# Retention and a two-layer PReLU network on one core: first batch in chunks of 128 tokens, second batch with one block of products for each pair of heads

## The chip, the cores and the metric

The kernel runs on one core of a Trainium2 chip. A core has TensorE (matrix products, written to PSUM banks), VectorE, ScalarE, GpSimd and a queue engine that starts transfers; they run beside each other and wait for one another by semaphores. The metric is the device time of one execution in microseconds. Everything is in fp32.

## What is computed

Eight batches, eight heads, 576 tokens of 64 values. Each head's attention is a retention: scores that decay with the distance of the tokens, nothing above the diagonal. Its output is laid out as 4608 tokens of 512 values and goes through a network of 512 to 2048 to 512 with a leaky activation whose slope is different for each of the 2048 features.

```python
scores = q @ k.T / sqrt(64)                      # per batch and head, 576 x 576
gamma = 1 - 2.0 ** (-5 - h)
ret = scores * where(i >= j, gamma ** (i - j), 0)
x = (ret @ v)                                    # (8, 576, 8 * 64) -> 4608 x 512
h = x @ w_in                                     # 4608 x 2048
g = maximum(h, 0) + alpha * minimum(h, 0)
out = g @ w_out                                  # 4608 x 512
```

The retention is computed by chunks: inside a chunk by masked scores, and from earlier chunks through a running state, the sum of decayed k times v of each chunk (64 x 64 for each head).

## The kernel before

Batch 0 has its own path. It is cut into three parts, of 256, 256 and 64 tokens; a part of 256 tokens has four chunks of 64. All heads of a part are done together: transposes, scores, states, values. Here `c` is a pair of heads, `h2` a head of the pair, `m` one of two blocks of 128 tokens, and `p2` a chunk in the block. `half(x)` is partitions 64x to 64x + 63, `chunk(j)` is columns 64j to 64j + 63. q and k are scaled beforehand so that decay inside a part is a mere mask.

```python
def part_scores(x):
    ...
    banks = part_banks(x, 2 if x == 0 else None, "ps")
    for m in range(2):
        for c in range(NPAIR):
            for p2 in range(2):
                for h2 in range(2):
                    j = chunk(2 * m + p2)
                    nc.tensor.matmul(banks[h2][half(p2), (2 * c + m) * C:(2 * c + m + 1) * C],
                                     kT[half(h2), c, j], qT[half(h2), c, j], start=True, stop=True)
    # part 0: VectorE multiplies both banks by the mask; part 1: ScalarE copies, GpSimd masks

def part_states(x):            # four states of 64 tokens
    for m, c, p2, h2 in ...:
        nc.tensor.matmul(banks[p2][half(h2), m, c], kn[half(p2), m, 2 * c + h2],
                         vn[half(p2), m, 2 * c + h2], ...)
    # running sums over j = 0..3: part 0 by ScalarE copies and GpSimd, part 1 by VectorE

def part_values(x):
    for m, c, p2, h2 in ...:   # own chunk
        nc.tensor.matmul(banks[p2][half(h2 ^ p2), c, m], vn[half(p2), m, 2 * c + h2],
                         at[half(p2), h2, n * C:(n + 1) * C], ...)
    for j in range(1 if x == 0 else 0, 4):      # earlier chunks, in two halves of 32 partitions
        for c, h2, e in ...:
            nc.tensor.matmul(banks[j % 2][to:to + 32, c, j // 2],
                             su[half(h2), c, e:e + 32], qT[half(h2), c, chunk(j)], ...)
    # ScalarE copies to xb: for each j parity, the odd chunks with their heads swapped
```

After part 0 come filler products (`idle`), a small transpose for the slopes, and then the first unit of the network. A unit is 2 x 128 of the 2048 features for a block of 256 tokens: a first product `ph` (eight matmuls of 256 columns), the activation by ScalarE and VectorE, and a second product `po` (four matmuls of 512 columns). The first two blocks of tokens use this plain form; the others use seven products in place of eight (Strassen). The weights are rounded as they arrive, in 32 pieces, each with two operations of ScalarE, three of VectorE and one of GpSimd (`piece_in`, `piece_out`).

```python
idle = ps_h.tile([P, DM], FP32, tag="psh0", name="idle")
for _ in range(2):
    nc.tensor.matmul(idle, ident, part[0][0][:, 0]..., start=True, stop=True)
...                                             # slopes, weight pieces
plain_unit(0, 0)                                # ph of block 0, unit 0
plain_relu()
```

The pairs of heads of batch 1 (four pairs, n = 4 to 7) are spread over twelve plain units, in small steps between the units' products: "s" scores, "u" states and their running sums, "w" the copy of the sums, "p" scaling, "v" values, "t" transposes on VectorE.

```python
def pair_scores(n, kT, qT):
    ps = [ps_tile([P, NM, C], f"ps{p2}_{n}") for p2 in range(2)]
    for j in range(NJ):                         # nine chunks
        for h2 in range(2):
            nc.tensor.matmul(ps[j % 2][half(x), j // 2], kT[half(h2), chunk(j)], qT[half(h2), chunk(j)], ...)
    # ScalarE copies qT beside the scores, VectorE applies decay and mask
def pair_states(n, kn, vn):
    ps = [ps_tile([P, NM - 1, D], f"pu{p2}_{n}") for p2 in range(2)]
    for j in range(NJ - 1):
        for h2 in range(2):
            nc.tensor.matmul(ps[j % 2][half(x), j // 2], kn[half(1 - h2), j], vn[half(1 - h2), h2, j], ...)
    return running_sums(n, *ps)

for n, (kb, i) in enumerate(units):
    plain_unit(kb, i); plain_relu()
    if n >= 1: gap()                            # the next of the steps
    piece_in(1); piece_out(1)
    mlp_out()                                   # po of the unit before
    ...
    piece_in(1)
    if n >= 2: gap()
    piece_out(1)
```

Later batches do a pair in one block, `joint`: the values of the pair before, then `pair_front`, scores and states of eight chunks into two PSUM banks together, with the ninth chunk's scores in a bank of the values (`extra`).

Of the kernel before, what the change touches and what calls it, by code (L numbers as in the profile page):

```python
# [18 lines left out]
def kernel(  # L19
# [121 lines left out]
    def room(i, s0, n):  # L141
# [8 lines left out]
        ((5, 4), (5, 5), (5, 6), (6, 4)), ((6, 5), (6, 6), (7, 4), (7, 5)), ())]  # L150
# [32 lines left out]
    mask = const.tile([P, C], FP32, name="mask")  # L183
    nc.gpsimd.memset(mask, 1.0)
    for p2 in range(2):
        nc.gpsimd.affine_select(out=mask[p2 * C:(p2 + 1) * C], in_=mask[p2 * C:(p2 + 1) * C],
                                compare_op=ALU.is_ge, fill=0.0, base=0, pattern=[[1, C]],
                                channel_multiplier=-1)
# [208 lines left out]
    def plain_out(kb, i, g, between):  # L397
# [3 lines left out]
        for x in range(2):  # L401
            if x and between:
                between()
            for m in range(2):
                nc.tensor.matmul(acc[kb][m], g[:, 2 * x + m],  # L405
                                 w_out[i][:, 2 * x:2 * x + 2].rearrange("p x f -> p (x f)"),
                                 start=(i == 0 and x == 0), stop=(i == NU - 1 and x == 1))
# [140 lines left out]


    def pair_scores(n, kT, qT):  # L550
        c = pairs[n][1]

        mt = attn.tile([P, 2 * S], FP32, tag="at", name=f"mt_{n}").rearrange(
            "p (h j s) -> p h j s", h=2, s=C)
        ps = [ps_tile([P, NM, C], f"ps{p2}_{n}") for p2 in range(2)]
        for j in range(NJ):
            for h2 in range(2):
                x = (1 - h2, h2)[j % 2]
                nc.tensor.matmul(ps[j % 2][half(x), j // 2], kT[half(h2), chunk(j)],  # L559
                                 qT[half(h2), chunk(j)], start=True, stop=True)  # L560
        for h2 in range(2):
            nc.scalar.copy(mt[half(h2), h2].rearrange("p j s -> p (j s)"), qT[half(h2)])
        for p2 in range(2):
            for h2 in range(2):
                h, to, x = 2 * c + h2, half(1 - h2), (1 - h2, h2)[p2]
                nm = NM - p2
                nc.vector.scalar_tensor_tensor(
                    out=mt[to, h2, p2::2], in0=ps[p2][half(x), 0:nm], scalar=th[to, 3, h:h + 1],
                    in1=mask[to, None, :].to_broadcast([C, nm, C]), op0=ALU.mult, op1=ALU.mult)
        return mt  # L570

    def pair_states(n, kn, vn):
        ps = [ps_tile([P, NM - 1, D], f"pu{p2}_{n}") for p2 in range(2)]
        for j in range(NJ - 1):
            for h2 in range(2):
                x = (h2, 1 - h2)[j % 2]
                nc.tensor.matmul(ps[j % 2][half(x), j // 2], kn[half(1 - h2), j],  # L577
                                 vn[half(1 - h2), h2, j], start=True, stop=True)
        return running_sums(n, *ps)

# [22 lines left out]

    later = []

    def pair_front(n, kT, qT, kn, vn, extra):
# [20 lines left out]
        for h2 in range(2):  # L627
            to = half(1 - h2)
            nc.vector.scalar_tensor_tensor(  # L629
                out=mt[to, h2, NJ - 1], in0=extra[to],  # L630
                scalar=th[to, 3, 2 * c + h2:2 * c + h2 + 1], in1=mask[to],
                op0=ALU.mult, op1=ALU.mult)
        for p2 in range(2):
            for h2 in range(2):
# [4 lines left out]
                    in1=mask[to, None, :].to_broadcast([C, NM - 1, C]),  # L639
                    op0=ALU.mult, op1=ALU.mult)  # L640
        later.append(lambda: pair_sums(vn, running_sums(n, ps[0][:, 1], ps[1][:, 1])))
# [61 lines left out]

    def part_scores(x):
        at = tat[x] = (mlp.tile([P, 8 * P], FP32, tag="g", name=f"pa_{x}") if x == 0 else
                       room(4, 0, 4)).rearrange("p (h n) -> p h n", h=2)
        banks = part_banks(x, 2 if x == 0 else None, "ps")
        kT, qT = tT[x, 0], tT[x, 1]
        for m in range(2):
            for c in range(NPAIR):  # L710
                for p2 in range(2):
                    for h2 in range(2):
                        j = chunk(2 * m + p2)
                        nc.tensor.matmul(banks[h2][half(p2), (2 * c + m) * C:(2 * c + m + 1) * C],  # L714
                                         kT[half(h2), c, j], qT[half(h2), c, j],
                                         start=True, stop=True)
        for h2 in range(2):
            to, fro = [t.rearrange("p (n s) -> p n s", s=C) for t in (at[:, h2], banks[h2])]
            m = mask[:, None, :].to_broadcast([P, 8, C])
            if x == 0:  # L720
                nc.vector.tensor_tensor(out=to, in0=fro, in1=m, op=ALU.mult)
            else:
                nc.scalar.copy(to, fro)
                nc.gpsimd.tensor_tensor(out=to, in0=to, in1=m, op=ALU.mult)

    def part_states(x):
        kn, vn = part[x][0], part[x][2]
        banks = [t.rearrange("p (m c d) -> p m c d", m=2, c=NPAIR)
                 for t in part_banks(x, None if x == 0 else 0, "pu")]
        for m in range(2):  # L730
            for c in range(NPAIR):
                for p2 in range(2):
                    for h2 in range(2):
                        nc.tensor.matmul(banks[p2][half(h2), m, c], kn[half(p2), m, 2 * c + h2],  # L734
                                         vn[half(p2), m, 2 * c + h2],
                                         start=(m == 0 and c == 0),
                                         stop=(m == 1 and c == NPAIR - 1), skip_group_check=True)
        was = carry[x]
        for j in range(4):
            u = banks[j % 2][:, j // 2]  # L740
            if x == 0:
                nc.scalar.copy(sums[x][j], u)
                if j:
                    nc.gpsimd.tensor_tensor(out=sums[x][j], in0=was, in1=sums[x][j], op=ALU.add)
            else:
                nc.vector.tensor_tensor(out=sums[x][j], in0=was, in1=u, op=ALU.add)
            was = sums[x][j]

    def part_carry(x):
        nc.gpsimd.tensor_tensor(out=carry[x + 1], in0=sums[x][3],  # L750
                                in1=gch[:, 2, :, None].to_broadcast([P, NPAIR, D]), op=ALU.mult)

    def part_values(x):
        vn, qT, at = part[x][2], tT[x, 1], tat[x]
        banks = [t.rearrange("p (c m s) -> p c m s", c=NPAIR, m=2)
                 for t in part_banks(x, 0 if x == 0 else None, "pv")]
        for m in range(2):
            for c in range(NPAIR):
                for p2 in range(2):
                    for h2 in range(2):  # L760
                        n = 2 * c + m
                        nc.tensor.matmul(banks[p2][half(h2 ^ p2), c, m],
                                         vn[half(p2), m, 2 * c + h2],
                                         at[half(p2), h2, n * C:(n + 1) * C],
                                         start=(m == 0 and c == 0), stop=False,
                                         skip_group_check=True)
# [265 lines left out]
```

## Time and profile before

| | |
|---|---|
| median of 3 runs | 1011.64 us (1010.38 to 1014.41) |
| span of the profiled execution | 1008.5 us |
| TensorE busy | 995.2 us (99%) |
| VectorE busy | 773.4 us (77%) |
| ScalarE, GpSimd busy | 267.3 us, 179.0 us |
| DMA share, 0 to 25 and 25 to 50 us | 0.96, 0.98 |
| first unit's product starts | 19.63 us |
| steps of batch 1 | 73.7 to 148.1 us |

The page gives the busy time of each engine, then the chain of work that ended last, followed back from the last instruction to what released each step. Where the chain stays on one engine, that engine's own work sets the time; where it says "issue", the engine waited for nothing that the profile shows. The same chain can be listed in order of time, with each run of equal instructions as one line. The trace counts an fp32 product as two passes, each with its own load of weights.

### The profile page before, as it was taken

What the parts mean: (1) busy time and instruction counts of PE and PEld (TensorE: products, weight loads), DVE (VectorE), ACT (ScalarE), POOL (GpSimd) and SP (SyncE); (2) the same over time, 40 slices, a digit from 0 to 9 for tenths busy, and PEclk for the clock granted to TensorE, in tenths of its full rate; (3) what the DMA queues carried; (4) which work ended last, traced back from release to release, by engine and by line L of the source; (5) the groups of instructions that cost most, each with busy time, mean ns of one, the idle gap of its engine ahead of it and who ended that gap; (6) DMA issues with size and microseconds to landing.
All of it is one profiled execution on the core that took longest, in us unless ns stands there. A gap on an engine that the chain in (4) does not pass through costs nothing.

```text
span 1008.5 us, 23133 instructions
## 1 busy us (share of the span) xinstructions
PE 995.2 (99%) x9389; PEld 891.9 (88%) x9389; DVE 773.4 (77%) x2086; ACT 267.3 (27%) x605; POOL 179.0 (18%) x201
## 2 busy tenths in 40 slices
PE   6999999999999999999999999999999999999998
PEld 5666668999999999999999999999999999999997
DVE  7769968887878778687777788878788776666665
ACT  5656652322222222022022121222222210000000
POOL 5656674210200020100020000200010001010000
PEclk9999999999999999999999999999999999999999
DMA  9986744232322222031122222323222000000000
GB/s 236 252 194 150 182 74 109 49 72 48 69 48 65 53 42 63 13 69 31 40 48 51 40 52 44 70 48 69 48 43 52 13 22 1 22 1 22 1 22 22
DMA packets 229595, 64.30 MB, mean 64 GB/s; under 512 B 214368, under 2 KB 223088, under 8 KB 229488
## 3 DMA queue, kind: packets, MB, share of 16 engines
q1 hardware_dynamic: 227088, 62.02, 27.4%
q8 instruction: 74, 1.21, 0.5%
q10 hardware_dynamic: 2400, 0.79, 0.4%
q14 instruction: 33, 0.27, 0.1%
HBM read 53.35 MB, written 9.44 MB: 62 GB/s over the span
## 4 chain that ended last, share of the span: by engine, by line
PE 98%; DMA 1%; issue 0%; DVE 0%; ACT 0%; SPq 0%; DVEq 0%
PE ph L470 40%; PE po L388 38%; PE ph L426 6%; PE po L405 6%; PE pv L652 3%; PE ps L616 1%; PE ps L622 1%; DMA w_out<-in_k_dram 1%; PE pv L966 1%; PE pt L695 0%; PE ps L714 0%; PE pv L773 0%; PE ps L559 0%; PE pu L734 0%; PE pu L577 0%
## 5 line engine op out<-in xcount | busy, mean ns | idle before, releaser
L388 PE MATMUL po<-w_out,g 128*128 128x256 f32 x1792 | 408.1, 379 | 0.0
L388 PEld LDWEIGHTS po<-w_out,g 128*128 128x128 f32 x1792 | 330.7, 190 | 39.7
L481 DVE TENSOR_TENSOR g<-ph,g 128x256 f32<-128x256 f32 (+1 forms) x512 | 187.0, 386 | 134.0 <-PE ph L470 67.7
L470 PE MATMUL ph<-xb,w_in 128*128 128x128 f32 x2048 | 272.7, 276 | 0.0
L470 PEld LDWEIGHTS ph<-xb,w_in 128*128 128x128 f32 x2048 | 257.1, 192 | 7.4 <-issue 0.5
L470 PE MATMUL ph<-xt,w_in 128*128 128x128 f32 x1536 | 213.3, 275 | 0.0
L470 PEld LDWEIGHTS ph<-xt,w_in 128*128 128x128 f32 x1536 | 192.1, 192 | 0.0
L476 ACT COPY g<-ph 128x128 f32<-128x128 f32 x128 | 34.1, 266 | 404.4 <-PE ph L470 391.9
L492 DVE TENSOR_TENSOR g<-g 128x128 f32<-128x128 f32 x512 | 129.4, 293 | 7.0
L531 POOL TENSOR_TENSOR qx<-qx,tabx 128x576 f32<-128x576 f32 x28 | 32.7, 1168 | 353.2 <-DMA qx<-in_q_dram 180.1
L486 DVE SCALAR_TENSOR_TENSOR g<-g 128x512 f32<-128x512 f32 x128 | 89.8, 701 | 3.0
L484 DVE TENSOR_SCALAR g<-g,alpha 128x256 f32<-128x256 f32 x256 | 85.8, 377 | 3.7
L405 PE MATMUL po<-w_out,g 128*128 128x512 f32 x128 | 58.6, 599 | 0.8 <-DVE g L442 0.8
L426 PE MATMUL ph<-xb,w_in 128*128 128x256 f32 x256 | 58.6, 383 | 0.0
L663 ACT COPY xb<-pv 128x256 f32<-128x256 f32 (+3 forms) x84 | 23.2, 315 | 126.5 <-PE pv L652 126.5
L426 PEld LDWEIGHTS ph<-xb,w_in 128*128 128x128 f32 x256 | 47.9, 190 | 9.3 <-issue 2.4
L600 ACT COPY vn<-su 64x512 f32<-64x512 f32 x56 | 34.5, 616 | 78.3 <-DVE su L594 77.9
L636 DVE SCALAR_TENSOR_TENSOR mt<-ps,th,mask 64x256 f32<-64x256 f32 x96 | 46.4, 483 | 2.2
L456 POOL TENSOR_TENSOR xt<-xb 128x256 f32<-128x256 f32 x16 | 11.6, 727 | 196.9 <-PE ph L470 196.9
L405 PEld LDWEIGHTS po<-w_out,g 128*128 128x128 f32 x128 | 23.4, 190 | 24.4 <-issue 22.8
L629 DVE SCALAR_TENSOR_TENSOR mt<-pv,th,mask 64x64 f32<-64x64 f32 x48 | 13.6, 283 | 40.2 <-ACT xb L663 39.8
L536 ACT ACTIVATE vn<-vn,tabv 64x576 f32<-64x576 f32 x56 | 43.2, 772 | 1.8 <-DMA vn<-in_v_dram 0.5
(136 smaller groups left out, 737.9 us busy)
## 6 DMA issues: line engine op xcount, KB each, us to landing
out_dram<-osb SPq DMA_DIRECT2D x34, 256.0 KB, 2.1
kx<-in_k_dram SPq DMA_DIRECT2D x112, 72.0 KB, 2.5
qx<-in_q_dram SPq DMA_DIRECT2D x112, 72.0 KB, 2.9
vn<-in_v_dram SPq DMA_DIRECT2D x56, 144.0 KB, 3.3
kn<-in_k_dram SPq DMA_DIRECT2D x56, 144.0 KB, 3.8
raw<-in_moe_w_in_dram SPq DMA_DIRECT2D x24, 256.0 KB, 4.4
raw<-in_moe_w_out_dram SPq DMA_DIRECT2D x10, 512.0 KB, 4.5
w_in<-in_moe_w_out_dram SPq DMA_DIRECT2D x6, 512.0 KB, 5.6
```

The source lines that it names most:

```text
L388: nc.tensor.matmul(acc[kb][n // 2][:, n % 2, :], g[:, x, :], w_out[i][:, y, :], start=(i == 0 and n % 2 == 0), stop=(i == NU - 1 and (n % ...
L405: nc.tensor.matmul(acc[kb][m], g[:, 2 * x + m], w_out[i][:, 2 * x:2 * x + 2].rearrange("p x f -> p (x f)"), start=(i == 0 and x == 0), sto ...
L426: nc.tensor.matmul(ph[:, x], w_in[i // UST][:, cc // 2 * 2 + x, i % UST, cc % 2], xb[kb][:, cc], start=(cc == 0 and x == 0), stop=(cc == N ...
L470: nc.tensor.matmul(ph[m][:, o], w_in[i // UST][:, l, i % UST, cc], r[:, cc], start=(n in (0, 3) and cc == 0), stop=(n in (2, 6) and cc == ...
L476: nc.scalar.copy(g[:, 7], ph[0][:, 2])
L481: nc.vector.tensor_tensor(out=o, in0=x0, in1=x1, op=ALU.add)
L484: nc.vector.tensor_scalar(g[:, 4 + 2 * m:6 + 2 * m], g[:, 2 * m:2 * m + 2], 0.0, alpha[:, fc:fc + 1], ALU.min, ALU.mult)
L486: nc.vector.scalar_tensor_tensor(out=g[:, 0:4].rearrange("p x t -> p (x t)"), in0=g[:, 0:4].rearrange("p x t -> p (x t)"), scalar=0.0, in1 ...
L492: ins = nc.vector.tensor_tensor(out=g[:, o, :], in0=g[:, x0, :], in1=g[:, x1, :], op=op)
L536: nc.scalar.activation(vn[x, h2], vn[x, h2], ACTF.Copy, scale=tabv[x, c:c + 1])
L600: nc.scalar.copy(vn[half(h2), h2, 1:], su[half(h2)])
L636: nc.vector.scalar_tensor_tensor(out=mt[to, h2, p2:NJ - 1:2], in0=ps[p2][half(x), 0], scalar=th[to, 3, h:h + 1], in1=mask[to, None, :].to_ ...
```

## The change

Batch 0 is cut in chunks of 128 tokens, so that a part has two chunks and two states. Batch 1 uses the same joint block of scores and states as the later batches, and this block is put inside a unit's second product, before the last of its four matmuls. Code that was there twice falls away. It is meant to shorten the work of the start: fewer products, states and copies for batch 0, and fewer breaks in the stream of large products for batch 1. The wait on ScalarE that swapped the heads of odd chunks falls away too.

The core of the diff (shortened, cuts marked):

```diff
-    mask = const.tile([P, C], FP32, name="mask")
+    mask2 = const.tile([P, P], FP32, name="mask2")       # triangle of 128 x 128
...
 def plain_out(kb, i, g, between):
         for x in range(2):
-            if x and between:
-                between()
             for m in range(2):
+                if between and 2 * x + m == between[0]:
+                    between[1]()
                 nc.tensor.matmul(acc[kb][m], g[:, 2 * x + m], ...)
...
 def part_scores(x):
         for m in range(2):
+            to = slice(m * P, (m + 1) * P)
             for c in range(NPAIR):
-                for p2 in range(2):
-                    for h2 in range(2):
-                        j = chunk(2 * m + p2)
-                        nc.tensor.matmul(banks[h2][half(p2), ...], kT[half(h2), c, j], qT[half(h2), c, j], ...)
+                for h2 in range(2):
+                    nc.tensor.matmul(banks[h2][m][:, c * P:(c + 1) * P], kT[half(h2), c, to],
+                                     qT[half(h2), c, to], start=True, stop=True)
+    def part_masks(x, banks, h2):
+        for m in range(2):
+            if h2 == 0:
+                nc.vector.tensor_tensor(out=to, in0=fro, in1=w, op=ALU.mult)
             else:
                 nc.scalar.copy(to, fro)
+                nc.gpsimd.tensor_tensor(out=to, in0=to, in1=w, op=ALU.mult)
...
 def part_states(x):
         for m in range(2):
             for c in range(NPAIR):
-                for p2 in range(2):
-                    for h2 in range(2):
-                        nc.tensor.matmul(banks[p2][half(h2), m, c], kn[half(p2), m, 2 * c + h2], ...)
+                for h2 in range(2):
+                    nc.tensor.matmul(u[half(h2), m, c], kn[:, m, 2 * c + h2], vn[:, m, 2 * c + h2], ...)
...
 def part_values(x):
+        for h2 in range(2):
+            for m in range(2):
+                for c in range(NPAIR):
+                    nc.tensor.matmul(banks[m][half(h2), c], vn[:, m, 2 * c + h2],
+                                     at[h2][:, c, m * P:(m + 1) * P], ...)
+        for m in range(2):
+            ...                                            # part 0 has no earlier state for m = 0
+            for c in range(NPAIR):
+                for h2 in range(2):
+                    nc.tensor.matmul(banks[m][half(h2), c], su[m][half(h2), c],
+                                     qT[half(h2), c, m * P:(m + 1) * P], ...)
         for c in (slice(0, 2), slice(2, 4)) if x == 0 else (slice(0, NPAIR),):
-            nc.scalar.copy(to[:, 0, c], banks[0][:, c])
-            for h2 in range(2):
-                nc.scalar.copy(to[half(h2), 1, c], banks[1][half(1 - h2), c])
+            for m in range(2):
+                nc.scalar.copy(xb[x][:, c, m * P:(m + 1) * P], banks[m][:, c])
...
-    for _ in range(2):
+    for _ in range(3):
         nc.tensor.matmul(idle, ident, ...)
...
+    def amid(n):
+        extra = ps_h.tile([P, C], FP32, tag="psh0", name=f"pe_{n}")
+        last_chunk(n, extra)
+        pair_front(n, *turned.pop(n), loaded[n][0], loaded[n][3], extra)
+    for n, at in zip(range(NPAIR, last + 1), (2, 4, 7, 9)):
+        fronts[at] = n
+        after[at] = (("u", n),)
+        before[at + 1] = (("w", n), ("p", n + 1))
+        after[at + 1] = (("v", n), ("t", n + 1))
...
         piece_in(1)
-        piece_out(1)
-        mlp_out()
+        if n in fronts:
+            mlp_out((3, lambda: amid(fronts[n])))
+            piece_out(1)
+        else:
+            piece_out(1)
+            mlp_out()
```

`pair_scores` and `pair_states` are removed; the tag `psh0` of the ninth chunk's bank is the one that the first product of a plain unit uses. The own-chunk loop of `part_values` before ran over block, pair, chunk and head, with the head innermost; now the head is outermost.

## The prediction, written before the changed kernel was run

> **What bounds the kernel now.** I read the page first: the busy times, then the chain that ended last.
>
> ```profile
> span 1008.5 us, 23133 instructions
> ...
> PE 995.2 (99%) x9389; PEld 891.9 (88%) x9389; DVE 773.4 (77%) x2086; ACT 267.3 (27%) x605; POOL 179.0 (18%) x201
> ...
> PE 98%; DMA 1%; issue 0%; DVE 0%; ACT 0%; SPq 0%; DVEq 0%
> PE ph L470 40%; PE po L388 38%; PE ph L426 6%; PE po L405 6%; PE pv L652 3%; PE ps L616 1%; PE ps L622 1%; DMA w_out<-in_k_dram 1%; PE pv L966 1%; PE pt L695 0%; PE ps L714 0%; PE pv L773 0%; PE ps L559 0%; PE pu L734 0%; PE pu L577 0%
> ```
>
> TensorE is 98% of the chain, and the lines that the change touches (L714, L734, L762, L773 for the first batch, L559 and L577 for the second) are about 1% of it. Whatever happens is a matter of a few microseconds, and what counts is TensorE's own time there. The second view is the chain in order of time, from 7 to 45 us (start, length, what; "x64" counts passes, two for each fp32 product):
>
> ```profile
> 10.24 1.92 PE ps L714 x64
> 12.16 1.57 PE pu L734 x64
> 13.74 1.05 PE pv L762 x64
> 14.79 0.35 PE pv L773 x14
> 15.14 1.22 issue
> 16.35 1.21 PE pv L773 x77
> 17.56 1.91 PE idle L842 x4
> ...
> 29.64 1.09 PE ps L714 x64
> 30.73 0.93 PE pu L734 x62
> 31.66 0.83 issue
> 32.49 0.27 PE pu L734 x2
> ...
> 36.41 1.09 PE pv L762 x64
> 37.50 1.45 PE pv L773 x89
> 38.95 0.02 issue
> 38.97 0.60 ACT xb L779
> ```
>
> See that TensorE is the chain even here, that it stands still twice for "issue" (1.22 and 0.83 us), and once, about 0.66 us (0.02 + 0.60 + 0.04), for ScalarE's copy of the second part. The same view of the second batch:
>
> ```profile
> 73.71 0.73 PE ps L559 x36
> 74.44 3.63 PE po L405 x8
> 78.07 0.62 PE pu L577 x32
> 78.70 3.65 PE ph L426 x16
> 82.35 3.43 PE po L405 x8
> 85.78 1.20 PE pv L652 x36
> ```
>
> No wait at all; each small block also lengthens the large product after it by 0.2 us (3.63 and 3.65 against 3.43 and 3.45 undisturbed).
>
> **What the Trainium skill says.** "TensorEngine Tiling (Array Packing)", Key Properties: different tiles of the array run in parallel, and a change of the tiling mode drains the engine. The trace agrees. A pass of 128 columns on the full array takes 3.12/28 = 0.111 us, so 64 columns alone would take 0.056; the 64x64 products of L714 come every 1.09/64 = 0.017 us (over three at once), those of L652, which have 128 rows and alternate between two column halves, every 1.20/36 = 0.033 (under two at once). The 0.2 us after a block is the drain. "TensorE: Matmul & The Clock Gate", Part 1: the array runs at half clock until it has been busy for about 3.4 us. The trace's clock row shows nothing of it, but the same 64 passes took 1.92 us in the first part and 1.09 in the second, and the rate changes near 13.6 us, 3.4 after the first dense products. "Runtime: NRT & Kernel Launch", Instruction fetch mechanics: instructions come by DMA in blocks of 256. The two "issue" gaps lie 253 passes apart, each with its weight load, hence 506 instructions; I read them as late fetches while the DMA queues are full.
>
> **Part by part, first batch.** Each of the two parts (256 tokens) goes from four chunks of 64 to two of 128.
>
> Scores: 32 products of 64 columns on four tiles become 16 of 128 columns on two row halves, since the square above the diagonal is now computed and masked away. 32 passes x 0.111 / 2 = 1.78 us with a warm array. The second part: 1.78 + 0.1 of drain against 1.09, **+0.8**. In the cold first part times 1.92/1.09: 3.1 against 1.92, **+1.2**.
>
> States: 16 products over all 128 rows, alternating column halves: 32 x 0.033 = 1.07 us. First part against 1.57, **-0.5**. Second part against 0.93 + 0.83 + 0.27 = 2.03 with its gap. There are fewer passes ahead, so the first fetch gap (after 222 passes) should move from the first part's values to here; I leave 0.3 us for it: **-0.7**.
>
> Values, own chunk: 16 products with all 128 rows, 64 output partitions and 128 columns. The loop runs over the head outermost, so eight products in a row go to the same column half and nothing runs beside them: 32 x 0.111 = 3.56 us. Against 1.05 and 1.09: **+2.5** in each part. This is the largest term, and it rests on the order of the loop. The order is chosen because head 1's mask goes through ScalarE and GpSimd and comes late.
>
> Values from earlier states: first part 8 products, two at once: 16 x 0.111 / 2 = 0.9, with drain 1.1, against 0.35 + 1.21: **-0.5**. Second part 16 products, 1.8 with drain, against 1.45: **+0.4**.
>
> Gaps and filler: the 1.22 us gap leaves the first part, **-1.2**. The filler before the first unit grows from two products to three: 6 x 0.429 (a 512-column pass, 3.43/8) + 0.2 = 2.77 against 1.91, **+0.9**. In the second part the next transposes no longer use the bank that ScalarE empties, so that wait goes: **-0.7**.
>
> First part: 1.2 - 0.5 + 2.5 - 0.5 - 1.2 + 0.9 = +2.4. Second: 0.8 - 0.7 + 2.5 + 0.4 - 0.7 = +2.3. Together **+4.7 us** on TensorE's path.
>
> Beside it: ScalarE gets two copies of 0.59 us in the first part and loses two state copies (0.6) and two copies of values (0.7); GpSimd gets two mask products of 1.26 us and loses two sums of 0.75. The filler ran until 19.47 us and the last copy and the weights ended at 19.50 and 19.34; all of these move by a microsecond or so, TensorE by more, so I expect no wait there.
>
> **Second batch.** Per pair, before: 0.73 + 0.2 + 0.62 + 0.2 = 1.75 us for scores and states. The joint block that later pairs use already took 1.20 us plus 0.2 at 158.26 us, so 1.40: 0.35 saved, **-1.4** for four pairs. It is now put before the last of the four products of a unit's second product. Two things can wait. The block's ninth chunk takes the bank of the unit's first product, so it needs VectorE to have finished that unit's activation; and the next unit needs that bank back from VectorE. Three products are 3 x 0.858 = 2.57 us; VectorE finished the activation 2.0 to 3.3 us after the unit's products ended:
>
> ```profile
> 84.77 0.87 DVE L442 SCALAR_TENSOR_TENSOR g<-g,nalpha,ph 128x256 f32<-128x256 f32 x2
> ```
>
> here 85.64 against 82.35. And VectorE is nearly full in this stage. Five units hold ten weight pieces (2.14 us each, 77.82 to 79.96), five activations (0.8), and two pairs with masks (2 x 0.28 + 4 x 0.48 = 2.5), sums (2.9) and transposes (1.5): 21.4 + 4.0 + 13.8 = 39.2 us. TensorE would need 5 x 6.88 + 2 x 2.8 = 40.0. VectorE in strict order, with masks and sums now within one unit, makes the next activation late. I expect waits of 0.2 to 0.6 us at most pairs, **+1.4** in all, so a net of **0**.
>
> Sum: +4.7; from 1011.6 it gives **1016.3 us**.
>
> **Rivals.** First, the change is a gain. If eight products to one column half do overlap, or the fewer instructions matter more than the columns streamed, 2 x 1.8 of the values and part of the scores fall away; with the second batch's full -1.4 the time is near 1011. For it: the filler was lengthened, which makes sense only if TensorE comes to the first unit earlier. Against it: L652, which does alternate, is already bound by its columns (0.033 against 0.028 for two at once). Second, VectorE becomes the bound of the second batch: each of the four pairs waits 0.5 to 0.8 us twice, which adds 3 to 4 us in place of 1.4: 1019. For it: 39.2 against 40.0. Against: before, even its latest activation (85.64) came 1.3 us ahead of the next use of the bank (86.98). Third, the extra work is hidden, because the start waits for weights: the DMA share is 0.96 and 0.98 in the first 50 us. Then the first part's +2.4 would vanish: 1014. Against: in the chain TensorE waits for no DMA after 7.28 us, and the filler shows that what is waited for is less than 2 us away.
>
> **Range and chances.** The sum's spread is some 2 us on each side for overlap, 1 to 2 for waits, and the three runs before already lie 4 us apart. I take **1011.5 to 1020.5 us**. Two per cent is 20 us, more than the whole touched stage could give; **faster 0.01, within 0.97, slower 0.02**.
>
> **What would show it.** In the chain after: the first part's scores near 3 us with 32 passes; own-chunk values near 3.5 us in both parts, against 1.8 if they overlap; a filler of 2.8 us; the first unit's product at about 22 us against 19.63; no ScalarE wait before the transposes of the last chunk; joint blocks of 1.2 us in the second batch, with short VectorE waits around them; and from there the same steps of 3.12 and 3.02 us, some 5 us later. The prediction is wrong if the first unit starts before 20 us, or if TensorE waits long for VectorE or GpSimd between 60 and 150 us.

## The result: 1019.9 us, and the profile after

The changed kernel took **1019.91 us** (median of 4 runs, 1019.58 to 1020.01) against 1011.59 us before (median of 4, 1010.38 to 1014.41); the ratio is 1.0078, with a 95% interval of 1.0057 to 1.0099. It is slower by 0.8%, so within the 2%, and 3.6 us above the predicted 1016.3, near the upper end of the range. The profiled spans are 1018.1 and 1008.5 us: 9.6 us to account for. That is 1.3 us more than the medians differ, since the profiled run of before (1010.19 us) was faster than its median.

The head of the page after (span and busy times, as shown of before):

```profile
span 1018.1 us, 22392 instructions
...
PE 1002.7 (98%) x9023; PEld 898.6 (88%) x9023; DVE 774.0 (76%) x2094; ACT 266.2 (26%) x602; POOL 179.7 (18%) x200
```

741 instructions fewer, 366 of them on TensorE, and yet TensorE is busy 7.5 us longer. Here fewer instructions are not less work. The chain of waits, which carried the reading of before, now ends early: followed back from the last instruction it reaches only 151.75 us, where TensorE waits for a ScalarE copy. So the start is read from TensorE's timeline of after (start, length, line, product, passes; in brackets the idle time before and what ended it):

```profile
9.99 3.58 PE L694 MATMUL ps<-pT,pT 64*128 64x128 f32 x32
13.50 1.15 PE L721 MATMUL pu<-w_out,w_out 128*64 128x64 f32 x32
14.48 3.59 PE L747 MATMUL pv<-pa,w_out 128*64 128x128 f32 x32
...
19.03 2.84 PE L824 MATMUL idle<-w_out,ident 128*128 128x512 f32 x6
...
22.02 3.69 PE L429 MATMUL ph<-xb,w_in 128*128 128x256 f32 x16
...
43.95 0.71 PE L769 MATMUL pt<-ident,w_out 64*128 64x64 f32 x8
```

Scores, states, own-chunk values, the values of earlier states (18.00 to 19.03, left out above) and the filler follow each other without an issue gap. The first unit starts at 22.02 us against 19.62 in the timeline of before, and in the second part the transposes (43.95) follow the values without a wait for ScalarE. The second view is that of TensorE's waits, between 60 and 170 us. In that stretch it lists none for the kernel before; after (total, times, longest):

```profile
PE ph L429 <- DVE g L445: 2.1, 4, 0.8
PE pe L581 <- DVE g L445: 1.3, 2, 0.7
PE pv L630 <- ACT vn L570: 1.0, 3, 0.4
```

These are 4.4 us. The timeline shows more: the values of a pair take 1.20 us where they wait for nothing, and took 1.6 to 2.4 us here, which is 2.0 us over four pairs that this view does not list. A table made by subtracting start times in the two timelines (from each landmark to the next):

| stretch of TensorE's timeline | before | after | difference | predicted |
|---|---|---|---|---|
| scores of part 0 to the first unit (`ph`) | 10.17 to 19.62 | 9.99 to 22.02 | +2.6, less 0.2 by the earlier start | +2.4 |
| first unit to the scores of part 1 | 19.62 to 29.57 | 22.02 to 31.97 | 0.0 | 0 |
| scores of part 1 to the next `po` | 29.57 to 40.24 | 31.97 to 44.59 | +1.95 | +2.3 |
| from there to `ph` of unit 2 (batch 1 begins) | 40.24 to 70.09 | 44.59 to 74.44 | 0.0 | 0 |
| unit 2 to the first Strassen product | 70.09 to 151.54 | 74.44 to 161.21 | **+5.3** | 0 |
| from there to the end | 857.0 | 856.9 | -0.1 | 0 |

The two ends of the largest row, in the timeline of before and then of after:

```profile
70.09 3.62 PE L426 MATMUL ph<-xb,w_in 128*128 128x256 f32 x16
...
151.54 1.05 PE L470 MATMUL ph<-xb,w_in 128*128 128x128 f32 x8
```

```profile
74.44 3.62 PE L429 MATMUL ph<-xb,w_in 128*128 128x256 f32 x16
...
161.21 1.05 PE L473 MATMUL ph<-xb,w_in 128*128 128x128 f32 x8
```

So in these profiles batch 0 did what was predicted, and batch 1 is where the prediction was short.

### The profile page after: what moved, and what is told of

Same layout as the page of the kernel before. It is cut to its first block, busy times and chain, and to the rows that moved or that the text cites. A ratio compares the mean times of both kernels' runs of the same rounds, so it can differ in the third digit from the quotient of the medians.

```text
span 1018.1 us, 22392 instructions
## 1 busy us (share of the span) xinstructions
PE 1002.7 (98%) x9023; PEld 898.6 (88%) x9023; DVE 774.0 (76%) x2094; ACT 266.2 (26%) x602; POOL 179.7 (18%) x200
## 4 chain that ended last, share of the span: by engine, by line
PE 84%; DVE 0%; ACT 0%; DVEq 0%; issue 0%; ACTq 0%
PE ph L473 40%; PE po L391 38%; PE pv L630 3%; PE ps L594 1%; PE ps L600 1%; PE po L408 1%; PE pv L581 1%; PE ph L429 0%; ACT vn L570 0%; DVE s L370 0%; DVE u L370 0%; DVE osb L371 0%; DVEq L1016 0%; DVE osb L370 0%; ACTq L570 0%
## 5 line engine op out<-in xcount | busy, mean ns | idle before, releaser
L391 PEld LDWEIGHTS po<-w_out,g 128*128 128x128 f32 x1792 | 330.7, 190 | 39.7
L614 DVE SCALAR_TENSOR_TENSOR mt<-ps,th,mask 64x256 f32<-64x256 f32 x112 | 54.1, 483 | 3.9 <-PE ps L600 1.5
L630 PEld LDWEIGHTS pv<-mt,vn 128*64 128x64 f32 x1008 | 32.6, 138 | 12.9 <-DVE g L495 7.6
```

Source lines behind the costliest of these rows:

```text
L391: nc.tensor.matmul(acc[kb][n // 2][:, n % 2, :], g[:, x, :], w_out[i][:, y, :], start=(i == 0 and n % 2 == 0), stop=(i == NU - 1 and (n % ...
L614: nc.vector.scalar_tensor_tensor(out=mt[to, h2, p2:NJ - 1:2], in0=ps[p2][half(x), 0], scalar=th[to, 3, h:h + 1], in1=mask(to)[:, None, :]. ...
L630: nc.tensor.matmul(pv[j >= j1][half(h2), j - (j1 if j >= j1 else 0)], vn[:, h2, j], mt[:, h2, j], start=True, stop=True)
```

## Experiments

**The halves apart.** Is all of batch 1's loss made there, or is some of it inherited from the later start of batch 0? Two kernels: batch 0 as changed with the steps of batch 1 as before, and the reverse.

```diff
 # e1_batch0_only: the changed kernel, with
-        mlp_out((3, lambda: amid(fronts[n])))
+        steps "s", "u", "w", "p", "v", "t" between the products, as before
```

> Only batch 0 is changed (chunks of 128, three filler products); batch 1 is as before. My account: the two halves of the change add up, and batch 0 costs 4.3 us: the first product of the network starts near 22.0 us and the second product of unit (0,1) near 44.6, as in the changed kernel, against 19.6 and 40.3 before; no wait of TensorE after 60 us; about 1015.9 us. Rival: batch 1's waits come from batch 0's later copies, masks and weight pieces on the other engines; then TensorE waits after 60 us here too, and the time is near 1019.

Measured 1014.04 us against 1010.62, ratio 1.0033 (1.0020 to 1.0045), span 1012.0, 3.5 us over the profile of before. The first unit started at 21.15 us and the next `po` at 43.73, each some 0.9 us ahead of what was expected: the scores of the first part took 2.43 us here and 3.58 in after. TensorE had no wait after 60 us, so nothing of batch 1's loss is inherited.

```diff
 # e2_batch1_only: the kernel before, with
-        steps "s", "u", "w", "p", "v", "t" between the products
+        mlp_out((3, lambda: amid(fronts[n])))          # and the steps placed as after
```

> Only batch 1 is changed (joint block inside a unit's second product); batch 0 is as before. My account: VectorE's order inside a pair of units makes TensorE wait about 7 us in all and the joint block saves 1.4, so the stage takes 5.4 us more: about 1017 us, the waits on VectorE for the bank of the unit's first product as in the changed kernel. Rival (waits inherited from batch 0): no waits, 1010.2 us.

Measured 1016.39 us against 1010.62, ratio 1.0058 (1.0042 to 1.0074), span 1014.5, 6.0 us over before. From unit 2 to the first Strassen product took 86.75 us, the same 5.3 more than the 81.45 of before, with the same 2.1, 1.3 and 1.0 us of waits. The two halves add up, 3.5 + 6.0 = 9.5 of 9.6 us in the profiles (by the medians 3.4 + 5.8 = 9.2 against 8.3, which the intervals allow), and batch 1 loses its 5.3 us on its own. The rest of the 6.0 lies in the start, which varies from run to run (see the last section).

**Why the own-chunk values cost 3.5 us.** A single run, the loop of part 1 alone with the head innermost again:

```diff
 # e3_heads_innermost: the changed kernel, part_values of part 1
-        for h2 in range(2): for m in range(2): for c in range(NPAIR):
+        for m in range(2): for c in range(NPAIR): for h2 in range(2):
```

> The changed kernel, but in the second part of batch 0 the values' products alternate between the heads, and so between the column halves of the array. My account: products to one column half run one after the other; alternating ones run two at once: 32 passes in 1.8 to 1.9 us in place of 3.5, and about 1.6 us off the span. Rival: the 128 columns streamed through 128 rows set the pace whatever the half; then the passes still take 3.5 us.

Measured 1018.34 us, span 1016.6, 1.5 less than after. The timeline of this kernel, own-chunk values of part 1, one row for a pass on each column half:

```profile
38.70 0.32 PE L747 MATMUL pv<-w_out,w_out 128*64 128x128 f32 x1
38.71 0.32 PE L747 MATMUL pv<-pa,w_out 128*64 128x128 f32 x1
38.86 0.27 PE L747 MATMUL pv<-w_out,w_out 128*64 128x128 f32 x1
38.87 0.27 PE L747 MATMUL pv<-pa,w_out 128*64 128x128 f32 x1
```

The passes start in twos, 0.01 us apart, the second two 0.16 us after the first, later ones every 0.11 us: the two halves run side by side. The 32 passes went from 38.70 to 40.60, 1.9 us in place of 3.3. What the outermost head costs is thus the serial run on one column half, as the prediction had it.

**The filler.** A single run of the changed kernel with one filler product:

```diff
 # e4_filler_1: the changed kernel
-    for _ in range(3):
+    for _ in range(1):
         nc.tensor.matmul(idle, ident, ...)
```

> The changed kernel with one filler product in place of three. My account: the first product of the network needs ScalarE's copies (done at 20.06 us) and, for its second half, the last weights from GpSimd (21.35); with one filler it starts near 20.3 us in place of 22.0, 1.7 us off the span. Rival A: the filler keeps the array's clock up; then the first products run slower by a few microseconds and nothing is gained. Rival B: what is waited for moves with it, since ScalarE and VectorE share their queues with weight pieces; then less than 0.5 us.

Measured 1017.06 us, span 1015.3, 2.8 less than after. From the start of the filler to the first unit took 17.77 to 19.05, 1.28 us against 2.99 after: no wait took the place of the two products left out, which makes 1.7 us. The other 1.1 is not the filler's: the scores of part 0, with the same code, took 2.17 us in this run and 3.58 in the profile of after.

The same question of the kernel before:

```diff
 # e8_before_filler_1: the kernel before
-    for _ in range(2):
+    for _ in range(1):
         nc.tensor.matmul(idle, ident, ...)
```

> The kernel before with one filler product instead of two ahead of the first unit. In the changed kernel the two products more were pure cost, since TensorE came late anyway. In the kernel before, the last copy and the last weights ended at 19.50 and 19.34 us and the filler at 19.47, so by my reading the filler there covers a wait: with one product TensorE stands still instead, first unit at 19.0 to 19.6 us against 19.63, and the time changes by less than 0.6 us. Rival (the filler is pure cost here too): the first unit at 18.8 us, time 0.86 us shorter.

Measured 1011.73 us against 1011.00, ratio 1.0010 (1.0003 to 1.0016). The first unit started at 19.05 us in place of 19.62, so the filler covered no wait of that length, against my reading. Yet the kernel was not faster but 0.7 us slower. In its profile TensorE stood still for "issue" by 1.65 us ahead of the second unit (0.83 before) and for 1.06 us more amid the values of part 1 (none there before), so the next `po` came at 41.29 against 40.24. Whether the filler itself does anything for these gaps stays open; one profile of each kernel doesn't show it, and two kernels further down, which differ in the filler alone, have the opposite sign.

**The issue gaps.** The prediction took them for late instruction fetches, at a fixed count of instructions. A test: 20 passes more on TensorE ahead of the scores of part 0 in the kernel before.

```diff
 # e9_shift: the kernel before, ahead of part_scores(0)
+    for y in range(10):
+        nc.tensor.matmul(shift[...], tT[...], tT[...], start=True, stop=True)   # 64 columns, result unused
```

> The kernel before, with ten more small products (20 passes of 64 columns) ahead of the first part's scores. It asks what the gaps called issue are. My account: a late fetch of instructions, so they stay at the same count of passes, near 222 and 475 from the start: the first gap then falls 20 passes earlier, at the end of the own-chunk values (after 58 of 64) and not after 14 passes of the next group. Rival: the gap is a wait for the running sums or a bank, and stays at the 14th pass of that group. The time grows by about 0.5 us.

TensorE's timeline of this kernel:

```profile
14.69 1.04 PE L762 MATMUL pv<-pa,w_out 64*64 64x64 f32 x56 [0.27 <-DVE pa L721]
16.97 0.34 PE L762 MATMUL pv<-pa,w_out 64*64 64x64 f32 x6 [1.24 <-issue]
...
31.64 0.86 PE L734 MATMUL pu<-w_out,w_out 64*64 64x64 f32 x42
33.02 0.57 PE L734 MATMUL pu<-w_out,w_out 64*64 64x64 f32 x22 [0.53 <-issue]
```

The first gap now lies 58 passes into L762 (two of them ahead of the rows shown), where before it came after all 64 of L762 and 14 of L773: 20 passes earlier. The second lies after 42 passes of L734, before after 62: 20 earlier too. In e8_before_filler_1, which has two passes fewer, the second gap lay after 64: two later. The gaps stay at a place in the stream of instructions, not at an operation. That fits a fetch in blocks of 256 instructions, as "Runtime: NRT & Kernel Launch", Instruction fetch mechanics, describes it; but that page calls its cost mostly hidden, and these gaps of 0.5 us and more are not. That the fetch is what comes late is argued from the count; no run shows the fetch itself.

**Batch 1: is it VectorE's lateness?** A single run of e2_batch1_only with three inner steps of the running sums on VectorE left out, for the pairs of batch 1. The output lacks these terms; the time is that of a VectorE with less to do.

```diff
 # e5_no_inner_sums: e2_batch1_only, running_sums of the pairs of batch 1
-        for j in range(3, NJ - 1, 2):
+        for j in ():                                   # batch 1 only
             nc.vector.scalar_tensor_tensor(out=su..., in0=su..., scalar=gch..., ...)
```

> As the run with only batch 1 changed, but for batch 1's pairs the three VectorE steps that carry the running sums over chunks 3, 5 and 7 are left out (the output for batch 1 then misses these terms). My account (VectorE's queue is what TensorE waits for): 1.5 to 2.2 us less on VectorE between the masks and the next activation, so the waits for the bank of the unit's first product after a pair's values (0.45 to 0.9 us each) go, and those for the copy of the sums too: 3 to 4.5 us less than 1014.5 of span, near 1010.5. Rival: the wait is for PSUM or ScalarE's queue, and VectorE's late finish is only its last link; then the span stays within 1 us.

Measured 1011.43 us, span 1009.7. Batch 1's stretch took 80.93 us against 86.75, and of the 4.4 us of waits 0.3 were left. So three steps of VectorE per pair, which take 1.5 to 2.4 us in the timeline of after, decide over 5.8 us of TensorE's time: the joint block is fine, and VectorE behind it is late.

**What makes VectorE late.** Its timeline in the changed kernel, for the pair whose block ran from 80.56 to 81.76 us:

```profile
80.94 0.58 DVE L607 SCALAR_TENSOR_TENSOR mt<-pe,th,mask 64x64 f32<-64x64 f32 x2 [0.86 <-PE pe L581]
81.89 1.99 DVE L614 SCALAR_TENSOR_TENSOR mt<-ps,th,mask 64x256 f32<-64x256 f32 x4 [0.36 <-PE ps L600]
83.80 0.68 DVE L310 TENSOR_SCALAR wc<-wa 128x512 f32<-128x512 f32 x1
...
85.97 0.98 DVE L558 SCALAR_TENSOR_TENSOR su<-su,gch,ps 64x256 f32<-64x256 f32 x2
...
88.68 0.69 DVE L310 TENSOR_SCALAR wc<-wa 128x512 f32<-128x512 f32 x1
...
90.74 0.86 DVE L445 SCALAR_TENSOR_TENSOR g<-g,nalpha,ph 128x256 f32<-128x256 f32 x2
```

Read it from below. The activation (L445) starts at 90.74, though its product was done at 86.17 (start of the next row of TensorE). Ahead of it in VectorE's order stand masks (from 80.94), a weight piece (83.80), the running sums (85.97) and another weight piece (88.68). And the masks began late: VectorE stood idle for 0.86 + 0.36 us, waiting for the block, while the weight piece behind them could have run. At the second and fourth block it is 0.52 + 0.37 us, so four pairs make 4.2 us of such idle time. Before, the masks started right behind an activation, because the scores were a step of their own and done (74.44) before it began:

```profile
74.87 0.87 DVE L442 SCALAR_TENSOR_TENSOR g<-g,nalpha,ph 128x256 f32<-128x256 f32 x2 [0.37 <-ACT ph L432]
75.78 2.13 DVE L567 SCALAR_TENSOR_TENSOR mt<-ps,th,mask 64x320 f32<-64x320 f32 x4
```

In the changed kernel, on TensorE's side, the next product then waits for the activation at 90.74:

```profile
89.70 1.61 PE L630 MATMUL pv<-mt,vn 128*64 128x64 f32 x36
91.75 3.69 PE L429 MATMUL ph<-xb,w_in 128*128 128x256 f32 x16 [0.45 <-DVE g L445]
...
98.65 0.27 PE L581 MATMUL pe<-qT,kT 64*64 64x64 f32 x2 [0.63 <-DVE g L445]
```

The values take 1.61 us for 36 passes in place of 1.27, since the copies of the sums come late as well (ScalarE's two copies start at 88.86 and take 1.26 us), and the next pair's block waits again.

If order is the cause, another order should be the cure. First attempt, a single run: the last weight piece goes behind the activation.

```diff
 # e6_late_piece: e2_batch1_only; in the unit of a block and the next one
+        if n - 1 in fronts:
+            piece_out(1)                               # behind the next activation
...
-        piece_out(1)
+        if n not in fronts:
+            piece_out(1)
```

> As the run with only batch 1 changed, with the same work, but the last weight piece of a unit with a joint block goes behind the next unit's activation in VectorE's queue. My account (order, not amount): the activation after a pair comes 2.1 us earlier, so the waits of the next first product after the values go (three or four of about 0.9 us with what lies around them), those ahead of the joint block stay: span near 1012 against 1014.5. Rival (amount: VectorE is full, 39.2 of 40.0 us): the wait only moves to the joint block and the span stays within 0.7 us.

Measured 1020.78 us, span 1019.0; the stretch took 87.55 us. The span missed the expected 1012 by 7 us. TensorE's waits in this kernel:

```profile
PE pv L659 <- ACT vn L600: 2.7, 6, 1.0
PE pe L609 <- ACT mt L633: 2.2, 2, 1.1
```

The waits for the activation fell from 2.1 to 0.3 us, and more than that came back as waits for the sums' copies and for the masks. The activation was put ahead, but the idle time ahead of the masks (0.86 and 0.36 us, unchanged in its timeline) and the piece between masks and sums stayed. In batch 1 that is 0.8 us more than in e2_batch1_only, close to what the rival expected: the waits moved. The rest of the miss lies ahead of batch 1, where this run had issue gaps of 1.50 and 2.14 us.

Second attempt: a piece goes ahead of the masks, where VectorE stood idle, and the running sums directly behind the masks.

```diff
 # e10_order: e2_batch1_only
+        if n - 1 in fronts or n in fronts:
+            piece_out(1)                               # ahead of the masks
         mlp_out((3, lambda: amid(fronts[n])))
+            for x in after.pop(n): step(*x)            # sums right behind the masks
+            piece_out(1)
...
-        piece_out(1)
+        if n not in fronts and n + 1 not in fronts:
+            piece_out(1)
```

> As the run with only batch 1 changed, with three moves in VectorE's queue: running sums directly behind the masks, and the last piece of a unit with a joint block, and of the unit ahead of one, behind the next activation. My account (order): all waits on VectorE and on the copy of the sums fall below 0.5 us each, the 1.4 us of the joint block come out, and the time is 1009 to 1010.5 us, level with before or just under it. Rival (amount): waits of 3 us or more remain, 1013 us or more.

Measured 1013.94 us against 1011.16, ratio 1.0029 (1.0020 to 1.0038); the stretch took 83.48 us. That is 3.3 us better than e2_batch1_only, but the time is the rival's, above 1013 us. All waits of batch 1 that the view lists were gone but one of 2.30 us, which the expectation had not seen: ahead of the product at 114.85 us. VectorE's timeline of this kernel there:

```profile
111.10 0.78 DVE L542 STREAM_TRANSPOSE qT<-qx 128x576 f32<-128x576 f32 x1 [1.99 <-POOL qx L531]
111.80 0.67 DVE L307 TENSOR_SCALAR wc<-wa 128x512 f32<-128x512 f32 x1
...
113.84 0.86 DVE L442 SCALAR_TENSOR_TENSOR g<-g,nalpha,ph 128x256 f32<-128x256 f32 x2
```

The same pattern again: VectorE waits 1.99 us for GpSimd, whose queue holds work on weights ahead of the scaling of q, and then does a weight piece (111.80) ahead of the activation (113.84) that TensorE needs. So this one piece was moved behind that activation as well, with a filler of one product:

```diff
 # e12_candidate: e10_order, and
-        if n - 1 in fronts or n in fronts:
+        if n - 1 in fronts or n in fronts or n == 6:
             piece_out(1)
...
-        if n not in fronts and n + 1 not in fronts:
+        if n not in fronts and n + 1 not in fronts and n != 5:
             piece_out(1)
...
-    for _ in range(2):
+    for _ in range(1):
         nc.tensor.matmul(idle, ident, ...)
```

> First batch as in the kernel before, with a filler of one product instead of two; second batch with the joint block, VectorE's order of e10_order, and one weight piece more (the last one of the unit after a pair's block, ahead of the second pair's block) put behind the activation. Theory (batch 1 costs nothing once VectorE's queue is in the right order): the one wait of 2.30 us that e10_order still had falls below 0.5 us, from the first product after the first pair's start to the first Strassen product 81.2 to 81.7 us (before 81.45, e10_order 83.48), so the second batch ends level with before; the shorter filler gives 0 to 0.8 us in the first part. Time within 1 us of before, 1009.5 to 1011.5, and the interval of the ratio touches 1. Rival (VectorE has no room for the joint block in any order): the wait appears at another place, batch 1 stays above 83 us and the time is about 1013 to 1014.

Measured 1010.96 us against 1011.00, ratio 1.0001 (0.9993 to 1.0009). The stretch took 81.40 us, the 2.30 us wait became 0.23. VectorE's timeline of this kernel shows the order that works, at the first block:

```profile
78.52 0.68 DVE L307 TENSOR_SCALAR wc<-wa 128x512 f32<-128x512 f32 x1
...
80.69 0.58 DVE L636 SCALAR_TENSOR_TENSOR mt<-pe,th,mask 64x64 f32<-64x64 f32 x2
...
83.22 0.97 DVE L588 SCALAR_TENSOR_TENSOR su<-su,gch,ps 64x256 f32<-64x256 f32 x2
84.22 0.92 DVE L592 SCALAR_TENSOR_TENSOR su<-su,gch 128x64 f32<-128x64 f32 x3
...
87.45 0.86 DVE L442 SCALAR_TENSOR_TENSOR g<-g,nalpha,ph 128x256 f32<-128x256 f32 x2
```

A weight piece (78.52), the masks behind it without idle time (80.69), the sums, a piece, and the next activation at 87.45 us. That is 2.6 us after its product ended (84.88), as in the kernel before. VectorE is not idle less: it stood still for 2.62 us ahead of the activation before that piece, where TensorE was busy with another product.

The new order did one thing more. Its three sum steps (L592) took 0.92 us, where those of the changed kernel took 1.46 with products of GpSimd beside them:

```profile
86.07 1.29 POOL L317 TENSOR_TENSOR w_in<-w_in,raw 128x512 int32<-128x512 int32 x1 [4.06 <-DVE w_in L315]
...
86.98 1.46 DVE L562 SCALAR_TENSOR_TENSOR su<-su,gch 128x64 f32<-128x64 f32 x3
...
87.31 0.73 POOL L327 TENSOR_TENSOR w_out<-w_out 128x256 f32<-128x256 f32 x1
```

Over four pairs, a step took 0.28 us with no GpSimd product beside it and 0.46 to 1.19 us with one: 7.0 us for the twelve steps in after (6.9 in before), 3.4 in e12_candidate, where none met one. So VectorE's busy time in the stretch fell as well, from 70.2 us to 66.5. The runs don't tell what each part of the new order is worth; e5_no_inner_sums lost its waits with the idle time ahead of the masks unchanged.

Then the same with the filler of two, so that only batch 1 differs from before:

```diff
 # e13_order_filler_2: e12_candidate
-    for _ in range(1):
+    for _ in range(2):
         nc.tensor.matmul(idle, ident, ...)
```

> e12_candidate with the filler of two products that the kernel before has, so that only batch 1 differs from before. e12_candidate came out level with before (1010.96 against 1011.00 us) though its shorter filler, alone in e8_before_filler_1, cost 0.7 us. Theory (the two add up): the joint block in the right order is worth about 0.7 us, and the time is about 0.7 us under before, ratio 0.9993, with 81.2 to 81.6 us from the first product after the first pair's start to the first Strassen product. Rival (the 0.7 us of the shorter filler was chance of the start-up, as its own interval almost reaches 1): the ratio is within 0.0005 of 1.

Measured 1011.59 us against 1010.68, ratio 1.0007 (0.9999 to 1.0015); the stretch took 81.39 us. The expected 0.7 us below before did not come, and the ratio is also just outside the rival's 0.0005, though its interval is not. Against e12_candidate, which differs in the filler alone, the longer filler looks 0.6 us slower where e8_before_filler_1 had made it look 0.7 us faster, so neither is shown to be the filler's. Its profiled span is 1008.7 us against 1008.5: level. So the joint block in the best order found is worth nothing that can be measured, and no version here beats the kernel before.

**Is it the place inside the product?** A single run, with the order of e2_batch1_only, the block behind the whole second product:

```diff
 # e7_block_after: e2_batch1_only
-            mlp_out((3, lambda: amid(fronts[n])))
+            mlp_out()
+            amid(fronts[n])
```

> Second batch as changed (first batch as before), but the joint block is put after the whole second product of its unit, not ahead of its last quarter. The waits ahead of the block (0.6 and 0.7 us for the second and fourth pair) vanish, since VectorE has 0.86 us more to free the bank for the ninth chunk. But the same bank goes to the next unit's product right after, and VectorE must first read the ninth chunk (masks of both heads) out of it: the next product should wait 1 to 2 us after each of the four blocks. Theory (the place inside the product is what makes the bank come back in time): batch 1 gets 3 to 6 us longer than the 86.75 us of e2_batch1_only. Rival (the place doesn't matter, only VectorE's total work does): within 1 us of 86.75.

Measured 1018.50 us, span 1016.8; the stretch took 88.72 us, 2.0 more than e2_batch1_only, so neither what the theory nor what the rival gave. The waits ahead of the block vanished, as expected. But the next product followed each block at once: VectorE had read the ninth chunk out of the bank at 79.09 us, ahead of the end of the block itself at 79.33. The bank's way back, which I had feared in the prediction too, is no bound here. What grew is the wait for the copies of the sums, 4.0 us over eight times: VectorE's idle time ahead of the masks rose from 0.86 to 1.72 us. A later block made a later VectorE.

## Why the prediction was right, and where it was short

The range held (1019.9 in 1011.5 to 1020.5), with 0.6 us to spare, and the time is within 2% as forecast. The centre was 3.6 us too low, and the step that failed is a single one.

**First batch, right.** By starts in the timelines, first part: scores +1.7 (predicted +1.2), states -0.65 (-0.5), own values +2.4 (+2.5), earlier-state values with the gap -1.75 (-1.7), filler +0.9 (+0.9). The scores' surplus is within the spread of the start: the same 32 passes took 2.17 to 3.58 us in four profiles, and in e1_batch0_only they cost 0.6 us more than before, not 1.7. The medians put batch 0 at +3.4 us (e1_batch0_only), against the predicted 4.7. Second part: scores +1.1 (+0.8), states -1.1 (-0.7, of which 0.3 for a gap that did not come), own values +2.2 (+2.5: where the heads change, some passes overlap), earlier values and the ScalarE wait together -0.3 (-0.3). The largest term was right for its reason: e3_heads_innermost took the serial run away and 1.4 us of the values with it. That agrees with what "TensorEngine Tiling (Array Packing)", Key Properties, says of different tiles in parallel; that products to one tile don't overlap, the runs show: 0.110 us a pass against 0.06 a pass side by side.

**Second batch, the block: right. The waits: short.** The block amid the second product took 4.82 us with its host (77.90 to 82.72) against 3.43 undisturbed (71.01 to 74.44), so 1.39, where 1.40 was predicted: 1.4 us saved over four pairs. The term "waits of 0.2 to 0.6 us at most pairs, +1.4 in all" was the one mis-sized: 5.3 + 1.4 = **6.7 us**, of which 4.4 are in the view of waits and 2.0 in the values. The prediction had named a long wait for VectorE between 60 and 150 us as a sign of being wrong, and for this part it was. The second rival had it better, at 3 to 4 us, and named the right engine. Its arguments, 39.2 us of work for VectorE in 40.0, were on the page; what was weighed against it, that the activation came 1.3 us early before, said nothing of the order after. The sum of work asks whether VectorE can keep up on average. It could: e12_candidate has all the work, VectorE busy for 66.5 of 81.4 us. What the sum left out is the order. VectorE's timelines run through its queue in order, and in after it stands idle for 0.9 to 1.2 us ahead of each block's masks, with other work queued behind. With the order changed (e12_candidate, e13_order_filler_2) the prediction's net 0 came true, at 81.4 us against 81.45, with sum steps that no longer met GpSimd's products. Even then most of the block's saving is spent: the product after each block starts 0.1 to 0.2 us late and takes 0.1 longer than in e2_batch1_only, and one wait of 0.2 us is left. At all four blocks of e12_candidate that product starts 0.05 to 0.14 us after VectorE has read the ninth chunk out of the bank that the product needs (81.27 and 81.32 us at the first), so in this order the bank's way back is the likely bound; no run tests it.

**The other rivals.** A gain by overlap falls with the serial passes. That the start's extra work hides behind the weights falls too: e1_batch0_only is 3.4 us slower, and the shorter filler of e4_filler_1 brought the first unit forward with no wait in its place. Something of it holds in the kernel before: in one profile e8_before_filler_1 got its 0.6 us at the first unit and lost more in later gaps.

## What to carry to other kernels

When steps are joined to save breaks on the bounding engine, write down the in-order queue of the engine that takes up the results, item by item, and look for the item that now waits with ready work behind it; here an order with 0.9 to 1.2 us of such idle time per block cost 6.7 us, and the block saved 1.4. Total load against total time (39.2 of 40.0 us) did not decide it: the same work fitted in another order. Look also at what runs beside a step, since the same sum step took 0.28 us or up to 1.19. And before counting columns, look which tile each product goes to: the same passes took 3.3 us with the head outermost and 1.9 with it innermost.

## What the runs showed that was not expected

- The slow start of TensorE does not end at a fixed point. The same 32 score passes took 3.58 us in after, 3.46 in e3_heads_innermost, 2.43 in e1_batch0_only and 2.17 in e4_filler_1, while the page's clock row shows nine tenths or more throughout. A single profile of the start is good to 1.4 us at best.
- After issue gaps of 1.84, 2.12 and 2.39 us (e5_no_inner_sums, e7_block_after, e10_order) the filler's four passes took 3.68, 3.68 and 3.27 us in place of 1.98, up to twice as long; after gaps of 1.50 and 1.76 us (e6_late_piece, e13_order_filler_2) they took 1.98. "TensorE: Matmul & The Clock Gate", Part 1, has the slow rate come back after an idle window of about 3.4 us; here a gap of 1.84 us was enough. Whether the small products around the gap count as idle is not shown.
- The gaps for "issue" are tied to the instruction count (20 passes more, 20 passes earlier), but their lengths are not: at the same places they took 1.22 and 0.83 us in before, 1.76 and none in e13_order_filler_2, 0.82 and 3.03 in e12_candidate. What varies less is where the first one ends: at 16.35 to 17.07 us in all ten profiles that have it. Runs of one kernel lie up to 5 us apart (before, 1009.21 to 1014.47); these gaps are large enough for much of that, though only profiled runs show them.
